# Attention scores of two experts side by side in 64-row TensorE tiles, without copied queries, in a decay-attention plus mixture-of-attention kernel

## The chip, the cores and the metric

The kernel runs on one core of one Trainium2 chip. A core has a matrix engine (TensorE, PE in the profile, with its weight loads shown as PEld), three elementwise engines (VectorE or DVE, ScalarE or ACT, GpSimd or POOL), a queue engine that here only issues transfers (SyncE or SP), an on-chip store of 128 partitions (SBUF) and eight accumulator banks of 128 partitions by 512 floats (PSUM). The metric is the device time of one launch in microseconds, as the median over runs. The time before is 322.6 us (three runs, 321.46 to 324.16).

## The reference, cut to what matters

```python
# 1. decay attention: 4 batches, 8 heads, 768 steps, 48 wide
for t in range(S):
    y[:, :, t] = rt @ (state + u * kt (x) vt)
    state = w * state + kt (x) vt
x = y as (4, 768, 384)
# 2. four experts of causal attention, 64 wide, two of four chosen per row
logits = x @ w_gate; topk = 2 best; w = softmax over them
for e in range(4):
    q, k, v = x @ wq[e], x @ wk[e], x @ wv[e]
    a = softmax(causal(0.125 * q @ k.T))
    out += [e in topk] * w_e * (a @ v @ wo[e])
```

Everything is float32. Where one TensorE pass at reduced precision would lose too much, the kernel splits a number into a rounded high part and the rest, a low part, and adds the products of the parts.

## The kernel before, in words

The 4 x 768 rows are cut into 24 chunks of 128 rows (n = 0 to 23). Three chunks make a group G (0 to 7, 384 rows); each batch has two groups, g = G % 2. The decay attention works by chunks (functions named a_...), the experts by groups (m_...).

For each chunk the decay attention ends in `a_add`, which leaves the 128 x 384 output. `a_xt` (lines 628 to 638) turns it on TensorE so that the 384 features lie on partitions: three columns of 128, read with a step of three floats, each in two halves of 64 rows (line 634, six transposes, the halves in two PSUM banks). ScalarE copies them out as the high part (line 637), and `a_xl` leaves the low part (line 645).

`m_proj(G, kind, pr)` (lines 666 to 698) computes queries (kind 0) or keys (kind 1) of the two experts 2 pr and 2 pr + 1 for a group: nine products of 384 columns (line 676), the first expert's 64 features on partitions 0 to 63, the second's on 64 to 127. Keys go to a tile of their own for each expert which holds the high part on the expert's own 64 partitions and the low part on the other 64: two copies on ScalarE (line 686) and two subtractions on VectorE (line 688), each on 64 partitions. Queries are split into high and low parts in the tile xq (lines 691 and 693), and then four transfers (line 698, on the SP queue) copy them so that each expert's query tile tq holds the same 64 features on both halves of the partitions.

`m_scores(G, e, j)` (lines 753 to 773) computes the scores of one expert for one chunk of queries against all N keys up to its end, N = 128 (3 g + j + 1). Because the key tile has high and low parts stacked, a single product over 128 partitions gives query x (high + low). It takes two: with the query's high part (line 763) and with its low part (line 764). For N of 640 and 768 each is cut into 384 columns and the rest. VectorE adds the causal mask and takes the row minimum in one instruction (line 770), and ScalarE takes the exponential and its sum (line 772). `m_weigh` scales the rows on GpSimd (line 785), `m_turn` turns them in halves of 64 rows (line 794), `m_av` multiplies by values (line 815), `m_out` projects to the output (lines 838 to 852). `m_values` (line 711) and `m_gate` give values and the gate.

Nothing here is scheduled while it runs. `ORDER` (line 16 on) is an order of the whole program written out: each word names a step and its arguments, and stands once for each stretch of that step between two `yield`s; the digits behind the slash say which buffers that stretch takes. The loop at line 863 goes through the words and issues the instructions in just that sequence, and each engine executes its own in that sequence. The eight PSUM banks are shared: `ps` number i is bank i, `psb` number i is banks i and i + 1 (`SHARED`, line 198).

Instructions on TensorE come in several shapes of the array: products over all 128 rows and 128 columns (lines 676, 711, 763, 764, 838 to 840), 64 rows by 128 columns (transposes in halves, lines 527, 634, 794), 64 by 64 (lines 566, 574, 599, 603) and 128 by 64 (line 815). The profile writes them as 128*128, 64*128, 64*64 and 128*64.

## Time and profile before

| | |
|---|---|
| median of three runs | 322.6 us (321.46 to 324.16) |
| the profiled execution's own time | 323.65 us |
| span of the profiled execution | 321.9 us |
| TensorE busy | 310.4 us (96%), 5406 products |
| VectorE, ScalarE, GpSimd busy | 214.8 us, 223.1 us, 174.3 us |
| transfers | 37.41 MB in 104698 packets |

Busy times overlap between engines. A product's record on TensorE is longer than the time it holds the engine, since the next one starts before the last has left the array; the pace of products that follow each other is therefore read from the distance between the ends of neighbours, or from the chain of waits, which counts each stretch once. Rows of a grouped view read: line, engine, operation, output and inputs, shape, count, then busy time and mean duration in ns, then idle time before them. Rows of the timeline read: start in us, length in us, engine, line, operation, count. Rows of the chain read: start, length, what.

### The profile page before, as it was taken

How to read it: one execution, taken by the hardware profiler on the slowest of the kernel's cores; microseconds unless marked ns; L12 is line 12 of the kernel's file. 1: busy time of each engine (PE TensorE's matmuls, PEld its weight loads, DVE VectorE, ACT ScalarE, POOL GpSimd, SP SyncE). 2: the span in 40 equal slices, each digit the busy share in tenths (PEclk: the TensorE clock that was granted, in tenths of full speed). 3: DMA queues.
4: the chain of work that ended last, by engine and by line, in shares of the span. 5: the costliest groups of instructions: out<-in, count | busy, mean ns of one | idle time of the engine just before them, and what ended most of it. 6: DMA issues, size and time to landing. Idle time of an engine off the chain costs nothing.

```text
span 321.9 us, 12990 instructions
## 1 busy us (share of the span) xinstructions
PE 310.4 (96%) x5406; PEld 264.7 (82%) x5407; DVE 214.8 (67%) x693; ACT 223.1 (69%) x525; POOL 174.3 (54%) x227
## 2 busy tenths in 40 slices
...
GB/s 168 223 176 104 100 197 115 148 178 170 117 82 180 180 57 119 195 134 2 150 108 152 53 126 70 166 190 73 77 89 100 170 27 4 124 145 30 25 51 73
DMA packets 104698, 37.41 MB, mean 116 GB/s; under 512 B 95550, under 2 KB 100544, under 8 KB 104640
## 3 DMA queue, kind: packets, MB, share of 16 engines
...
q14 instruction: 16, 0.13, 0.1%
q10 hardware_dynamic: 160, 0.10, 0.1%
...
## 4 chain that ended last, share of the span: by engine, by line
PE 89%; ACT 4%; DVE 3%; issue 2%; DMA 1%; ACTq 0%; DVEq 0%
PE banks L676 16%; PE banks L815 12%; PE banks L711 9%; PE banks L763 8%; PE banks L794 8%; PE banks L764 6%; PE banks L566 4%; PE banks L603 3%; PE banks L527 3%; PE banks L634 3%; PE banks L838 3%; PE banks L599 3%; PE banks L574 3%; PE banks L840 3%; PE banks L839 3%
## 5 line engine op out<-in xcount | busy, mean ns | idle before, releaser
L785 POOL TENSOR_SCALAR pr<-pr,f,gate 128x128 f32<-128x128 f32 (+5 forms) x96 | 67.8, 723 | 79.7 <-DVE f L779 35.6
L770 DVE CUSTOM_DVE_ANT_0 pr<-banks,after 128x256 f32<-128x256 f32 (+5 forms) x96 | 58.6, 620 | 37.2 <-PE banks L764 28.6
L772 ACT ACTIVATE pr<-pr,nm 128x384 f32<-128x384 f32 (+5 forms) x96 | 63.5, 663 | 19.9 <-DVE nm L770 17.9
L797 ACT ACTIVATE pt<-banks 128x768 f32<-128x768 f32 (+1 forms) x64 | 44.5, 729 | 8.5 <-PE banks L794 8.3
L763 PE MATMUL banks<-tk,tq 128*128 128x384 f32 (+3 forms) x128 | 45.0, 355 | 0.1
L815 PE MATMUL banks<-pt,vv 128*64 128x384 f32 (+2 forms) x324 | 40.4, 393 | 1.0 <-DVE yl L824 0.7
L764 PE MATMUL banks<-tk,tq 128*128 128x384 f32 (+3 forms) x128 | 40.4, 322 | 0.0
L815 PEld LDWEIGHTS banks<-pt,vv 128*64 128x64 f32 x324 | 20.6, 136 | 17.5 <-issue 12.8
L676 PE MATMUL banks<-xt_hi,wqk_lo 128*128 128x384 f32 x96 | 32.5, 338 | 0.5 <-issue 0.5
L676 PE MATMUL banks<-xt_hi,wqk_hi 128*128 128x384 f32 x96 | 32.9, 342 | 0.0
L794 PEld LDWEIGHTS banks<-ident,pr 64*128 64x128 f32 x672 | 24.7, 139 | 9.5 <-issue 4.4
L676 PE MATMUL banks<-xt_lo,wqk_hi 128*128 128x384 f32 x96 | 32.3, 336 | 0.0
L794 PE MATMUL banks<-ident,pr 64*128 64x64 f32 x672 | 30.2, 229 | 0.8 <-ACT pt L797 0.6
L626 POOL TENSOR_TENSOR z<-z,w 128x192 f32<-128x192 f32 x20 | 10.2, 509 | 34.5 <-DVE z L622 34.5
L763 PEld LDWEIGHTS banks<-tk,tq 128*128 128x128 f32 x128 | 24.0, 187 | 3.7 <-ACT vv L716 0.3
L490 POOL TENSOR_TENSOR rdbuf<-rdbuf,tab_r 128x384 f32<-128x384 f32 x22 | 23.1, 1053 | 7.1 <-DMA rdbuf<-in_r_dram 5.1
L497 POOL TENSOR_TENSOR ku<-kdbuf,uw 128x384 f32<-128x384 f32 x24 | 25.0, 1046 | 0.4
L490 POOL TENSOR_TENSOR kdbuf<-kdbuf,tab_k 128x384 f32<-128x384 f32 x21 | 22.3, 1063 | 5.3 <-DMA kdbuf<-in_k_dram 5.2
L499 POOL TENSOR_TENSOR ku<-ku,rdbuf 128x384 f32<-128x384 f32 x24 | 24.5, 1023 | 1.3
L599 PE MATMUL banks<-vsbuf,sm 64*64 64x48 f32 x384 | 23.9, 220 | 0.5 <-issue 0.3
L764 PEld LDWEIGHTS banks<-tk,tq 128*128 128x128 f32 x128 | 24.1, 188 | 0.3
L599 PE MATMUL banks<-vhbuf,sm 64*64 64x48 f32 x384 | 23.9, 219 | 0.0
...
## 6 DMA issues: line engine op xcount, KB each, us to landing
tq<-xq SPq DMA_DIRECT2D x64, 192.0 KB, 3.4
kdbuf<-in_k_dram SPq DMA_DIRECT2D x24, 192.0 KB, 3.6
vhbuf<-in_v_dram SPq DMA_DIRECT2D x24, 192.0 KB, 3.8
rdbuf<-in_r_dram SPq DMA_DIRECT2D x24, 192.0 KB, 3.7
out_dram<-o SPq DMA_DIRECT2D x23, 192.0 KB, 2.5
...
pr<-in_moe_wo_dram SPq DMA_DIRECT2D x2, 192.0 KB
...
```

Of the source, the lines that this page charges most:

```text
L490: nc.gpsimd.tensor_tensor(t[:, :, :D], t[:, :, :D], (tab_k, tab_r)[which], op=OP.mult)
L599: nc.tensor.matmul(o, st["sm", n][par][rows, p // 2, i], values, start=fresh, stop=True)
L676: nc.tensor.matmul(ps, a[:, t, m0:m0 + P], x[:, t, :], start=i == 0, stop=i == n - 1)
L711: nc.tensor.matmul(ps, x[:, t, cols], a[:, t, :], start=m == 0, stop=m == n - 1)
L763: nc.tensor.matmul(o, tq[:, 0, q], keys[:, n0:n1], start=True, stop=False)
L764: nc.tensor.matmul(o, tq[:, 1, q], keys[:, n0:n1], start=False, stop=True)
L770: nc.vector.tensor_tensor_reduce(pr[:, :N], ps, after[:, S - N:], 1.0, 3e38, op0=OP.add, op1=OP.min, accum_out=nm)
L772: nc.scalar.activation(pr[:, :N], pr[:, :N], AF.Exp, bias=nm, scale=-1.0, accum_out=sums[:, e, j, 0:1])
L785: nc.gpsimd.tensor_scalar(p[:, :N], p[:, :N], f[:, i], gate[:, i, e:e + 1], op0=OP.mult, op1=OP.mult)
L794: nc.tensor.transpose(both[:, x, half], mg[G]["p", e, j][rows, i * C:(i + 1) * C], ident[rows, rows])
L797: nc.scalar.activation(pt.rearrange("s (x half c) -> s x half c", x=n, half=2), both, AF.Copy)
L815: nc.tensor.matmul(psy[par * HD:par * HD + HD, j0 * C:j1 * C], vv[:, i % GC, e, :], mg[G]["t", e, i][:, (j0 - max(0, i - g * GC)) * C:(j1 ...
```

## The change

`m_scores` now takes a pair of experts at once. Keys and queries keep the layout in which `m_proj` leaves them, the pair's experts on the two halves of the partitions, with high and low parts as two tiles side by side. For each stretch of keys there are three products for each expert (high x high, high x low, low x high; low x low is dropped), each over 64 partitions, and those of the two experts alternate, each expert writing to its own bank or pair of banks. The four transfers for queries and the tile xq are gone, and keys take one copy and one subtraction over 128 partitions in place of two each over 64. `a_xt` turns the whole 128 rows at once, three transposes into one bank. There are eight probability tiles in place of six and three query tiles (of a pair) in place of four (of an expert). The order of the whole program is laid anew; of its text only the end is shown here, then all of the rest of the diff.

```diff
--- before.py
+++ after.py
...
-m_turn,7,0,0/4 m_av,6,0,0,3/1 m_scores,7,1,0/0 m_av,6,0,0,3/0 m_out,5,1/0 m_turn,7,0,0/3 m_scores,7,1,0/14
-m_scores,7,1,0 m_scores,7,1,1/1 m_scores,7,1,1/05 m_scores,7,1,1 m_proj,7,0,1/31 m_scores,7,2,2/6 m_out,5,0 m_proj,7,1,1
-m_turn,7,0,1/4 m_turn,7,0,2/0 m_turn,7,0,1/2 m_weigh,7,1/1 m_weigh,7,1 m_av,6,1,0,3/2 m_av,6,1,0,3/0 m_scores,7,2,0/3
-m_scores,7,2,2/43 m_scores,7,2,1/5 m_turn,7,0,2/0 m_av,6,1,0,3/1 m_out,6,0/7 m_scores,7,2,2 m_turn,7,1,0/0
-m_scores,7,2,1/11 m_scores,7,2,1 m_turn,7,1,0/5 m_turn,7,1,1/5 m_turn,7,1,1/1 m_scores,7,2,0/02 m_out,6,0/1
-m_scores,7,3,0/4 m_scores,7,3,2/2 m_turn,7,1,2/0 m_scores,7,3,2/44 m_out,5,1 m_scores,7,2,0 m_scores,7,3,0/50
-m_scores,7,3,2 m_out,6,0 m_weigh,7,2/2 m_out,6,2/5 m_weigh,7,2 m_scores,7,3,1/6 m_scores,7,3,0 m_out,6,1/2
-m_scores,7,3,1/25 m_scores,7,3,1 m_weigh,7,3/0 m_weigh,7,3 m_av,7,0,0,3/3 m_turn,7,1,2/4 a_sum,17 m_turn,7,2,1/0
-m_out,6,1/0 m_out,6,1 m_turn,7,2,0/6 m_out,6,2/1 m_turn,7,2,1/3 m_turn,7,2,0/5 m_av,7,0,3,6 m_av,7,0,3,6/1
-m_turn,7,3,0/4 m_turn,7,3,2/6 m_turn,7,3,1/0 m_turn,7,3,0/0 m_turn,7,2,2/4 m_turn,7,3,1/2 m_turn,7,2,2/4 m_turn,7,3,2/1
-m_av,7,1,3,6/1 m_av,7,1,3,6/0 m_av,7,0,3,6/1 m_av,7,1,3,6/0 m_out,7,0/3 m_av,7,1,3,6 m_av,7,1,3,6 m_out,7,1/7 m_out,6,2
-m_av,7,1,3,6 m_out,7,0/0 m_out,7,1/1 m_av,7,1,3,6 m_out,7,2/2 m_out,7,0 m_out,7,1 m_out,7,2/1 m_out,7,2/0 m_out,7,2/1
-m_out,7,2
...
+m_turn,6,3,0/4 m_gate,7/300 m_proj,7,1,0 m_proj,7,0,1/0 m_proj,7,0,1 m_gate,7 m_scores,7,0,0/03 m_scores,7,0,0/46
+m_scores,7,0,0/35 m_scores,7,0,1/16 m_turn,6,3,0/2 m_out,5,0/0 m_scores,7,0,1/54 m_scores,7,0,1/21 m_scores,7,0,2/31
+m_scores,7,0,2/02 m_weigh,6,2 m_turn,6,2,0/5 m_scores,7,0,0 m_scores,7,0,0 m_scores,7,0,1 m_out,5,1/7 m_out,5,0/1
+m_scores,7,0,2/50 m_turn,6,2,0/1 m_out,4,0 m_scores,7,0,2 m_scores,7,0,2 m_gate,7/600 m_weigh,7,0/0 m_out,5,2/0
+m_scores,7,0,1 m_weigh,7,1/3 m_proj,7,1,1/2 m_proj,7,1,1 m_out,5,0 m_av,6,0,0,3/3 m_out,5,1/0 m_out,5,1 m_out,5,2/1
+m_av,6,0,0,3/0 m_proj,7,1,1 m_scores,7,1,2/64 m_weigh,7,0 m_weigh,7,1 m_turn,7,0,1/0 m_turn,7,0,1/5 m_av,6,1,0,3/2
+m_scores,7,1,2/23 m_scores,7,1,2/57 m_scores,7,1,2 m_av,6,0,0,3/0 m_turn,7,0,0/6 m_turn,7,1,1/0 m_turn,7,0,0/1
+m_turn,7,1,1/4 m_scores,7,1,0/45 m_turn,7,0,2/6 m_turn,7,0,2/0 m_av,6,1,0,3/1 m_turn,7,1,0/0 m_scores,7,1,0/16
+m_scores,7,1,0/42 m_scores,7,1,0 m_av,6,1,0,3/1 m_scores,7,1,1/63 m_out,6,1/5 a_sum,5 m_turn,7,1,0/3 m_scores,7,1,1/34
+m_scores,7,1,1/05 m_out,6,0/1 m_scores,7,1,1 m_out,5,2 m_scores,7,1,0 m_scores,7,1,1 m_out,6,2/2 m_weigh,7,2/2
+m_weigh,7,2 m_turn,7,1,2/6 m_av,7,0,0,3/0 m_scores,7,1,2 m_weigh,7,3/3 m_weigh,7,3 m_out,6,0/0 m_turn,7,2,0/3
+m_turn,7,1,2/2 m_out,6,1/1 m_out,6,1 m_turn,7,2,0/1 m_turn,7,2,1/6 m_turn,7,2,1/3 m_av,7,0,3,6 m_av,7,0,3,6/1
+m_turn,7,3,0/3 m_turn,7,3,0/0 m_turn,7,3,1/5 m_turn,7,3,1/2 m_turn,7,3,2/3 m_av,7,0,3,6/0 m_turn,7,2,2/0 m_out,6,0
+m_turn,7,3,2/4 m_turn,7,2,2/5 m_av,7,1,3,6/7 m_out,6,2/1 m_av,7,1,3,6/0 m_av,7,1,3,6/1 m_out,7,0/5 m_av,7,1,3,6
+m_out,7,0/0 m_out,6,2 m_out,7,0 m_av,7,1,3,6 m_av,7,1,3,6 m_out,7,1/2 m_out,7,1/1 m_av,7,1,3,6 m_out,7,1 a_sum,17
+m_out,7,2/7 m_out,7,2/1 m_out,7,2/3 m_out,7,2/1 m_out,7,2
 """
 
 BUFS = {
-    "ps": 8, "psb": 7, "pr": 6, "tq": 4, "xq": 2, "pt": 6, "yh": 2, "yl": 2, "ku": 2, "ownv": 2, "kt": 2, "rt": 3, "rx": 3, "sm": 4, "z": 3, "o": 2,
+    "ps": 8, "psb": 7, "pr": 8, "tq": 3, "pt": 6, "yh": 2, "yl": 2, "ku": 2, "ownv": 2, "kt": 2, "rt": 3, "rx": 3, "sm": 4, "z": 3, "o": 2,
     "tk": 2, "vv": 3, "xt_hi": 2, "xt_lo": 2, "lg": 2, "gt": 2, "dl": 2, "ex": 2,
     "gate": 2, "nm": 6, "f": 4,
 }
 WIDTH = {
-    "ps": 512, "psb": 1024, "pr": 768, "tq": 768, "xq": 768, "pt": 768, "yh": 384, "yl": 384, "ku": 384, "ownv": 384,
+    "ps": 512, "psb": 1024, "pr": 768, "tq": 768, "pt": 768, "yh": 384, "yl": 384, "ku": 384, "ownv": 384,
     "kt": 512, "rt": 512, "rx": 256, "sm": 256, "z": 576, "o": 384, "tk": 3072, "vv": 768, "xt_hi": 1152, "xt_lo": 1152, "lg": 12, "gt": 48,
     "dl": 12, "ex": 12, "gate": 12, "nm": 1, "f": 3,
 }
 SHARED = {"ps": 512, "psb": 512}
-ROUNDED = ("tq", "xq", "yh", "yl", "tk", "xt_hi", "xt_lo")
+ROUNDED = ("tq", "yh", "yl", "tk", "xt_hi", "xt_lo")
 
 EARLY = 3
 
@@ -628,21 +616,19 @@
     def a_xt(n):
         G, j = divmod(n, GC)
         x = st["x", n]
-        ps = take("psb").rearrange("s (half x) -> s half x", half=2)[:, :, :KT * 64].rearrange("s half (t c) -> s t half c", t=KT)
+        ps = take("ps")[:, :KT * C].rearrange("s (t c) -> s t c", t=KT)
         for t in range(KT):
-            for half, rows in enumerate((lo, hi)):
-                nc.tensor.transpose(ps[:, t, half], x.rearrange("s (p t) -> s p t", t=KT)[rows, :, t], ident[rows, rows])
+            nc.tensor.transpose(ps[:, t, :], x.rearrange("s (p t) -> s p t", t=KT)[:, :, t], ident)
         cols = slice(j * C, (j + 1) * C)
         yield
-        nc.scalar.activation(turned("xt_hi", G)[:, :, cols].rearrange("s t (half c) -> s t half c", half=2), ps, AF.Copy)
+        nc.scalar.activation(turned("xt_hi", G)[:, :, cols], ps, AF.Copy)
         st["xt", n] = ps
 
     def a_xl(n):
         G, j = divmod(n, GC)
         hi, lo = turned("xt_hi", G), turned("xt_lo", G)
         cols = slice(j * C, (j + 1) * C)
-        halves = (x[:, :, cols].rearrange("s t (half c) -> s t half c", half=2) for x in (lo, hi.bitcast(F32)))
-        nc.vector.tensor_tensor(next(halves), st["xt", n], next(halves), op=OP.subtract)
+        nc.vector.tensor_tensor(lo[:, :, cols], st["xt", n], hi[:, :, cols].bitcast(F32), op=OP.subtract)
 
 
     sumsbuf = [const.tile([P, E, GC, 2], F32, name=f"sums{i}") for i in range(2)]
@@ -653,15 +639,14 @@
 
     mg = {G: {} for G in range(B * NG)}
 
-    def keys_of(G):
-        b, g = divmod(G, NG)
-        return get("tk", b).rearrange("s (e g c) -> s e g c", e=E, g=NG)[:, :, g]
+    def keys_of(b, pr):
+        return get("tk", b).rearrange("s (p i c) -> s p i c", p=E // 2, i=2)[:, pr]
 
     def values_of(G):
         return get("vv", G).rearrange("s (j e h) -> s j e h", j=GC, e=E)
 
-    def query_of(G, e):
-        return get("tq", G, e).rearrange("s (i c) -> s i c", i=2)
+    def query_of(G, pr):
+        return get("tq", G, pr).rearrange("s (i c) -> s i c", i=2)
 
     def m_proj(G, kind, pr):
 
@@ -676,26 +661,16 @@
                 nc.tensor.matmul(ps, a[:, t, m0:m0 + P], x[:, t, :], start=i == 0, stop=i == n - 1)
                 i += 1
         yield
-        top, bot = slice(0, 64), slice(64, 128)
         if kind:
-
-            tk = keys_of(G)
-            for e, own, other in ((2 * pr, top, bot), (2 * pr + 1, bot, top)):
-                if e % 2:
-                    yield
-                nc.scalar.activation(tk[own, e, :], ps[own], AF.Copy)
-                yield
-                nc.vector.tensor_tensor(tk[other, e, :], ps[own], tk[own, e, :].bitcast(F32), op=OP.subtract)
+            x2 = keys_of(b, pr)[:, :, g * GT:(g + 1) * GT]
+            nc.scalar.activation(x2[:, 0], ps, AF.Copy)
+            yield
+            nc.vector.tensor_tensor(x2[:, 1], ps, x2[:, 0].bitcast(F32), op=OP.subtract)
             return
-        x2 = take("xq").rearrange("s (i c) -> s i c", i=2)
+        x2 = query_of(G, pr)
         nc.scalar.activation(x2[:, 0], ps, AF.Copy, scale=-scale)
         yield
         nc.vector.scalar_tensor_tensor(x2[:, 1], ps, -scale, x2[:, 0].bitcast(F32), op0=OP.mult, op1=OP.subtract)
-        yield
-        for e, half in ((2 * pr, top), (2 * pr + 1, bot)):
-
-            for rows in (top, bot):
-                nc.sync.dma_start(query_of(G, e)[rows].bitcast(F32), x2[half].bitcast(F32))
 
     def logits_of(G):
         return get("lg", G).rearrange("p (c e) -> p c e", c=GC)
@@ -750,27 +725,28 @@
         nc.vector.tensor_tensor(gate, den.to_broadcast([P, GC, E]), ex, op=OP.mult)
         mg[G]["gate"] = gate
 
-    def m_scores(G, e, j):
+    def m_scores(G, pr, j):
         b, g = divmod(G, NG)
-        tq, sums = query_of(G, e), sumsbuf[G % 2]
+        tq, tk, sums = query_of(G, pr), keys_of(b, pr), sumsbuf[G % 2]
         N = (g * GC + j + 1) * C
-        psb = take("psb")
         q = slice(j * C, (j + 1) * C)
-        keys = get("tk", b).rearrange("s (e c) -> s e c", e=E)[:, e]
         first = 0 if N <= 512 else 512 - GT
+        ps = [take("ps" if N <= 512 else "psb")[:, first:first + N] for _ in range(2)]
         for n0, n1 in ((0, N),) if N <= 512 else ((0, GT), (GT, N)):
-            o = psb[:, first + n0:first + n1]
-            nc.tensor.matmul(o, tq[:, 0, q], keys[:, n0:n1], start=True, stop=False)
-            nc.tensor.matmul(o, tq[:, 1, q], keys[:, n0:n1], start=False, stop=True)
-        ps = psb[:, first:first + N]
-        yield
-
-        nm = take("nm")
-        pr = take("pr")
-        nc.vector.tensor_tensor_reduce(pr[:, :N], ps, after[:, S - N:], 1.0, 3e38, op0=OP.add, op1=OP.min, accum_out=nm)
-        yield
-        nc.scalar.activation(pr[:, :N], pr[:, :N], AF.Exp, bias=nm, scale=-1.0, accum_out=sums[:, e, j, 0:1])
-        mg[G]["p", e, j] = pr
+            for i, (part, key) in enumerate(((0, 0), (0, 1), (1, 0))):
+                for par, rows in enumerate((lo, hi)):
+                    nc.tensor.matmul(ps[par][:, n0:n1], tq[rows, part, q], tk[rows, key, n0:n1], start=i == 0, stop=i == 2)
+        prs = []
+        for par in range(2):
+            yield
+            nm, pr_ = take("nm"), take("pr")
+            nc.vector.tensor_tensor_reduce(pr_[:, :N], ps[par], after[:, S - N:], 1.0, 3e38, op0=OP.add, op1=OP.min, accum_out=nm)
+            prs.append((nm, pr_))
+        for par, (nm, pr_) in enumerate(prs):
+            yield
+            e = 2 * pr + par
+            nc.scalar.activation(pr_[:, :N], pr_[:, :N], AF.Exp, bias=nm, scale=-1.0, accum_out=sums[:, e, j, 0:1])
+            mg[G]["p", e, j] = pr_
 
     def m_weigh(G, e):
         g = G % NG
```

More of the change, by code (lines that the diff above doesn't have):

```diff
@@ new lines @@
+a_decay,11,0 a_quarters,9/4 a_sum,8/2 a_sum,9 m_scores,1,1,1 m_scores,1,1,1 a_sum,9/0 load_chunk,12 m_proj,2,1,0/7
+a_mask,9/03 a_sum,10 m_proj,2,1,0/1 a_ku,10/1 a_ku,10 load_vs,9 a_out,9 load_vs,12 load_chunk,13 load_chunk,13
+m_weigh,1,3/0 a_out,10 m_weigh,1,2/3 m_weigh,1,2 m_weigh,1,3 m_proj,2,0,1/3 m_proj,2,0,1/2 m_proj,2,1,1/6 a_own,10/0
+a_add,10 load_vh,13 a_xt,10/5 load_chunk,11 m_proj,2,1,0 a_add,9 m_proj,2,1,1 a_xt,9/2 a_decay,12,1 m_proj,2,1,1
+a_xt,9/1 a_xl,9/1 m_proj,2,0,0/1 a_xt,10 m_av,1,0,0,3/7 m_proj,2,0,1 m_turn,1,3,2/1 load_chunk,14 m_turn,1,3,2/3 a_ku,12
@@ new lines @@
+m_scores,2,1,2/05 m_scores,2,1,2/57 m_weigh,2,1/1 a_xt,11 a_xt,12/0 a_xt,12/0 a_decay,14,1 a_decay,14,0 a_transpose,14/2
+a_transpose,13/5 m_av,1,1,3,6/0 a_xl,12/0 a_transpose,14/0 a_decay,15,0 m_av,1,1,3,6/1 m_out,1,2/7 a_decay,15,1 a_xl,11
+m_proj,3,0,0/4 a_transpose,13/1 a_transpose,13/00 m_out,1,2/0 a_sum,11 m_weigh,2,1 m_turn,2,1,0/0 m_weigh,2,0/1
+m_weigh,2,0 m_turn,2,0,0/5 a_transpose,14/21 m_values,3,0/7 m_scores,2,1,1/23 m_scores,2,1,1/13 load_vh,14
+m_turn,2,1,0/3 load_chunk,16 a_decay,16,0 a_ku,14/1 a_ku,14 m_turn,2,0,0/1 m_values,3,0/0 load_chunk,16
@@ new lines @@
+m_turn,3,1,2/6 m_scores,3,1,1/46 m_proj,4,0,1/4 m_scores,3,1,1/32 m_out,2,0 m_scores,3,1,1 a_decay,19,1 m_weigh,3,2/3
+a_xt,15/2 m_proj,4,1,1 m_turn,3,1,2/5 load_vh,18 a_ku,16 a_xt,15/1 a_own,16/71 m_values,4,2/0 m_values,4,0/3
+m_values,4,0 m_scores,3,1,1 a_xl,15/1 m_values,4,2 m_values,4,2 m_out,2,2/1 m_out,0,0 m_proj,4,0,1/1 a_quarters,16/2
+m_proj,4,0,1 a_transpose,18/5 m_gate,4/000 m_scores,3,1,0 m_scores,3,1,2 m_weigh,3,3/1 m_av,3,0,0,3/4 a_sum,15/2
+load_chunk,20 a_sum,16 a_mask,16/31 m_values,4,0 m_out,2,2/1 a_ku,17/0 m_gate,4 m_gate,4/311 a_transpose,18/0
@@ new lines @@
+a_transpose,18/11 m_weigh,3,2 m_av,3,0,3,6 m_av,3,0,3,6/1 m_av,3,0,3,6/0 a_out,16 m_turn,3,2,2/0 a_ku,18/1
+m_turn,3,2,2/2 m_weigh,3,3 m_turn,3,2,1/5 m_turn,3,2,1/4 warm_up m_turn,3,3,0/3 m_turn,3,3,0/1 m_scores,4,0,1/10
+a_add,16 a_xt,16/7 a_xt,16 m_turn,3,3,2/5 m_turn,3,3,2/0 m_scores,4,0,1/51 m_scores,4,0,1/13 a_sum,16/1 m_turn,3,3,1/1
+m_turn,3,3,1/3 a_decay,20,0 m_turn,3,2,0/3 m_scores,4,0,0/05 a_xl,16 a_decay,17,1 a_transpose,17/6 a_ku,17
+m_scores,4,0,0/42 m_scores,4,0,0/25 m_scores,4,1,2/12 m_scores,4,1,2/37 m_scores,4,0,2/05 m_scores,4,0,2/00
```

277 lines of the change are left out of this document (121 added, 156 removed).

## The prediction

> **What bounds the kernel now.** I read the head of the page first, then busy time by stretches, then the chain of waits.
>
> ```profile
> span 321.9 us, 12990 instructions
> PE 310.4 (96%) x5406; PEld 264.7 (82%) x5407; DVE 214.8 (67%) x693; ACT 223.1 (69%) x525; POOL 174.3 (54%) x227
> PE 89%; ACT 4%; DVE 3%; issue 2%; DMA 1%; ACTq 0%; DVEq 0%
> PE banks L676 16%; PE banks L815 12%; PE banks L711 9%; PE banks L763 8%; PE banks L794 8%; PE banks L764 6%; PE banks L566 4%; PE banks L603 3%; PE banks L527 3%; PE banks L634 3%; PE banks L838 3%; PE banks L599 3%; PE banks L574 3%; PE banks L840 3%; PE banks L839 3%
> ```
>
> ```profile
> 12.00:40.00 28.00, 24.73 (x655) 21.88 (x655) 23.67 (x57) 20.79 (x49) 23.12 (x23) 1.00 0.64 144
> 40.00:312.00 272.00, 268.99 (x4646) 230.27 (x4645) 183.57 (x609) 197.14 (x466) 146.73 (x185) 1.00 0.50 113
> ```
>
> In the second view the columns after the length are PE, PEld, DVE, ACT, POOL busy, then the granted clock. From 40 to 312 us TensorE stands idle for 272.00 - 268.99 = 3.0 us; the next engine, ScalarE, is busy for 197 of 272. The chain agrees: 89% of it is TensorE. So work taken from TensorE shortens the span almost one for one, and work taken from VectorE, ScalarE or the transfers does nothing directly. The scores (lines 763 and 764) are 14% of the chain.
>
> **What a product costs.** Busy times overlap, so I take paces: the distance between the ends of neighbours in the timeline, and chain rows divided by their counts.
>
> ```profile
> 47.93 0.23 PE L763 MATMUL banks<-tk,tq 128*128 128x128 f32 x1
> 47.99 0.28 PE L764 MATMUL banks<-tk,tq 128*128 128x128 f32 x1
> ...
> 50.09 0.56 PE L634 MATMUL banks<-ident,ownv 64*128 64x64 f32 x6
> 50.57 0.39 PE L763 MATMUL banks<-tk,tq 128*128 128x256 f32 x1
> 50.80 0.28 PE L764 MATMUL banks<-tk,tq 128*128 128x256 f32 x1
> ```
>
> ```profile
> 299.08 0.35 PE L794 MATMUL banks<-ident,pr 64*128 64x64 f32 x6
> 299.36 0.50 PE L763 MATMUL banks<-tk,tq 128*128 128x512 f32 x1
> 299.70 0.40 PE L764 MATMUL banks<-tk,tq 128*128 128x512 f32 x1
> ```
>
> ```profile
> 60.43 1.57 PE banks L676 x9
> ...
> 63.95 0.50 PE banks L527 x16
> ...
> 66.69 0.52 PE banks L794 x12
> ```
>
> A product of 384 columns takes 1.57 / 9 = 0.174 us; of 512, from 299.86 to 300.10, 0.24; of 256, from 50.96 to 51.08, 0.12; of 128, from 48.16 to 48.27, 0.11. The last is as dear as twice its columns, so below 256 columns the weight load sets a floor of 0.11 for a step.
>
> A change of array shape costs more. At 50.57 the array goes from 64*128 to 128*128: from the end before (50.09 + 0.56 = 50.65) to that of the first product (50.96) is 0.31 against 0.12 for the next, 0.19 more. At 299.36 it is 0.43 against 0.24, again 0.19. Into 64*128: twelve transposes after L676 take 0.52, while sixteen within the shape take 0.50, or 0.031 each; 0.52 - 12 x 0.031 = 0.15.
>
> [...]
>
> **Scores.** By the code, each batch and expert has N = 128, 256, 384, 512, 384 + 256 and 384 + 384, two products each. Over 4 batches and 4 experts that is 128 products of 384 columns, 64 of 256, 32 of 128, 32 of 512: 128 x 0.174 + 64 x 0.12 + 32 x 0.11 + 32 x 0.24 = 22.3 + 7.7 + 3.5 + 7.7 = 41.2 us. Afterwards a pair needs three steps where it needed four products; if the two experts' products run side by side in their halves of the rows, and a step costs what a whole product of that width does, it is 96, 48, 24 and 24 steps, 30.9 us. Gain 10.3.
>
> Does a pair run side by side? The trace has no such product at reduced precision, but it has other work in halves and quarters of the array:
>
> ```profile
> 10.65 0.87 PE banks L407 x8
> ...
> 57.64 0.62 PE banks L566 x32
> ```
>
> ```profile
> L566 PEld LDWEIGHTS banks<-rt,kt 64*64 64x64 f32 x768 | 13.8, 134 | 3.1 <-issue 0.8 <-DVE kdbuf L488 0.5 <-DVE ownv L508 0.3
> L676 PEld LDWEIGHTS banks<-xt_hi,wqk_hi 128*128 128x128 f32 x96 | 18.0, 188 | 0.6 <-ACT vv L716 0.2
> ```
>
> A whole transpose of 128 x 128 takes 0.87 / 8 = 0.109; in two halves it takes 2 x 0.031 = 0.062, which two halves in turn, 0.054 each by their columns, would not reach. Ordinary products in quarters come every 0.62 / 32 = 0.019, under a quarter of the width's cost. In both the halves of the rows write to different banks, as the new scores do. So I take side by side. Bounds: nothing gained or lost per column (side by side, 30.9) and all in turn, 2 x 30.9 = 61.8; the nearest rows are near the first end.
>
> **Changes of shape.** Scores move from the whole shape to the one of the transposes in halves; `a_xt` the other way. I walked through both written orders and noted the shape of each step that issues to TensorE. Before: 67 changes into 128*128 (43 of them at scores), 63 into 64*128, 34 into 64*64, 18 into 128*64. Afterwards: 55, 59, 37, 19 (scores cause 19, `a_xt` 14, `m_proj` 13 instead of 3). 12 x 0.19 + 4 x 0.15 - 4 x 0.15 = 2.3; with the column shape, whose price I don't separate, 2.2 gained, bounds 1.8 to 2.5.
>
> **Turning whole.**
>
> ```profile
> 49.27 0.43 PEld L634 LDWEIGHTS banks<-ident,ownv 64*128 64x128 f32 x6
> ```
>
> ```profile
> L634 PEld LDWEIGHTS banks<-ident,ownv 64*128 64x128 f32 x144 | 10.2, 202 | 2.7 <-DVE ownv L610 0.7 <-issue 0.4 <-DVE tk L688 0.3
> L794 PEld LDWEIGHTS banks<-ident,pr 64*128 64x128 f32 x672 | 24.7, 139 | 9.5 <-issue 4.4 <-POOL pr L785 2.8 <-POOL kdbuf L490 0.6
> ```
>
> The six loads of a chunk come in three pairs, (0.43 - 0.20) / 2 = 0.12 apart, although the same transposes on contiguous data (L794) pace at 0.062 a pair: the load with a step of three floats, 0.202 long against 0.139, sets the pace. A whole transpose needs the same load once, and its own 0.109 can hide behind the next load, as loads hide in the run of L407. I take three steps of 0.12, as before: nothing. Bounds: 0.11 each (24 x 0.03 = 0.7 gained), and load and transpose end to end, 0.12 + 0.11 = 0.23 each, 24 x 3 x 0.11 = 7.9 lost; the overlap in L407 decides for the first.
>
> **Edits with no price.**
>
> ```profile
> L686 ACT ACTIVATE tk<-banks 64x384 fp32r<-64x384 f32 x32 | 15.2, 484 | 8.1 <-PE banks L676 7.0 <-DVE tk L688 0.6
> L688 DVE TENSOR_TENSOR tk<-banks,tk 64x384 fp32r<-64x384 f32 x32 | 17.4, 554 | 5.6 <-ACT tk L686 5.0
> L691 ACT ACTIVATE xq<-banks 128x384 fp32r<-128x384 f32 x16 | 7.8, 485 | 3.9 <-PE banks L676 3.7
> ```
>
> ```profile
> tq<-xq SPq DMA_DIRECT2D x64, 192.0 KB, 3.4
> ```
>
> A copy over 128 partitions (0.485) costs what one over 64 does (0.484), so keys lose 16 copies and 16 subtractions, 7.7 us of ScalarE and 8.9 of VectorE. The 64 query transfers go, with 3.4 us of latency each between projection and scores. All of this lies beside TensorE, which had 3.0 us of idle time to give; without that cover it would be worth at most those 3. In the new order the nearest scores (7,1,2) follow their projection with one `m_av` between, longer than the 0.485 + 0.554 that the split needs.
>
> **Waits of the new order.** The other engines keep 96% of their work while TensorE loses 4%, and a step of scores now fills two banks, or four, which one VectorE must empty.
>
> ```profile
> L770 DVE CUSTOM_DVE_ANT_0 pr<-banks,after 128x768 f32<-128x768 f32 x16 | 15.3, 956 | 7.4 <-PE banks L764 5.1 <-ACT pt L797 1.9 <-PE banks L794 0.4
> L770 DVE DVE_READ_ACCUMULATOR2_ANT nm<- 128x1 f32 x96 | 8.0, 83 | 0.0
> ```
>
> The second expert's banks are free 0.956 + 0.083 = 1.04 us later than the first's. I add half of the present idle time, 1.5 us; bounds -1.5 and 16.6 (all sixteen pairs of 640 and 768 keys wait that 1.04).
>
> **Sum.** -10.3 - 2.2 + 0 + 1.5 = -11.0 against the profiled execution's 323.65 us (span 321.9 and 1.75 around it): 312.65. That execution was 1.05 above the median of the runs, so for the median I forecast 311.6 us.
>
> **Rivals.**
>
> *Stalls at the banks* (0.14). The order may be tighter than its words show. Half of the 16.6 above, 8 us, gives 311.6 + 8 = 319.6. For: a pair of 640 or 768 keys takes four of eight banks, and two more are held by the values' sums. Against: VectorE was busy for 184 of 272 us and loses 8.9.
>
> *Weight loads exposed* (0.08), the one that ends slower. In each half of the rows the load for the next step would wait until the half's product is done. A step then costs load plus stream: 0.174 + 0.11 for 384, 0.23 for 256, 0.058 (a third of 0.174) + 0.11 for 128, 0.35 for 512, so 96 x 0.284 + 48 x 0.23 + 24 x 0.168 + 24 x 0.35 = 50.7 us of scores, 9.5 more than now; -2.2 + 1.5 besides gives 311.6 + 19.8 = 331.4. It decides as soon as a step of 384 columns costs over 0.26. Against: L676 paces at 0.174 with loads of 0.188 over the same rows, and L527 at 0.062 a pair, so loads hide behind products there. [...]
>
> *Halves in turn* (0.05). Reduced-precision products of two halves don't overlap: 61.8 us of scores, 311.6 + 30.9 = 342.5. For: no row shows such a product; against: L566 and L527.
>
> *Loads in turn* (0.05), the case in which the change does not bring what it says. The two loads of a step follow each other: a floor of 2 x 0.11 = 0.22 a step, 168 x 0.22 + 24 x 0.24 = 42.7, no gain over 41.2; 311.6 + 11.8 = 323.4. Against: L566 loads last 0.134 and come every 0.019.
>
> **How the numbers follow.** The forecast has 0.68, its own range 307 (more of the drains saved, no new waits, transposes at 0.11) to 315 (3 us more of waits). The range for 8 in 10 takes in the stalls and part of the dear transposes (up to 319.5): 307 to 321. About 1% is what a measurement of this kernel can tell from no change, so the lines are at 319.4 and 325.8. Faster: 0.68 and half of the stalls, 0.07, 0.75; same: the other half and loads in turn, 0.05, 0.12; slower: 0.08 + 0.05 = 0.13.
>
> **What would show it.** Right: steps of a pair of scores start together and pace at 0.17 to 0.18 for 384 columns; the score lines' share of the chain falls to about 10%; TensorE idle in the middle stays under 5 us; `a_xt` takes 0.33 to 0.37 us a chunk without its drain; 170 drains of 0.15 to 0.19 us remain. Wrong: a pace of 0.28 or 0.35, transposes at 0.23, or more than 10 us of TensorE idle before scores, named as waits for VectorE.

## The result, and the profile after

| | before | after |
|---|---|---|
| median of the runs taken together on one chip | 322.1 us (321.46 to 324.16) | 310.24 us (309.75 to 310.41) |
| profiled execution, own time | 323.65 us | 310.19 us |
| its span | 321.9 us | 308.5 us |

The ratio of the times (of their means) is 0.9619, with a 95% interval of 0.9572 to 0.9665. The forecast was 311.6 us with a range of 307 to 321. Runs of one kernel differ with the clock that TensorE was granted (the kernel before, run beside the experiments, took 321.64 us at a mean clock of 1.0 and 324.93 at 0.989), and where the runs of an experiment lie further apart than that, its ratio is that of the shorter ones.

The head of the page after, then the chain by engine and by line, which answer to the first fence of the prediction:

```profile
span 308.5 us, 12933 instructions
PE 298.6 (97%) x5463; PEld 253.6 (82%) x5463; DVE 202.8 (66%) x677; ACT 213.7 (69%) x509; POOL 173.8 (56%) x227
PE 90%; ACT 6%; issue 1%; DMA 1%; DVE 1%; ACTq 0%; DVEq 0%
PE banks L661 17%; PE banks L791 12%; PE banks L738 11%; PE banks L686 9%; PE banks L770 7%; PE banks L554 4%; PE banks L591 4%; PE banks L587 4%; PE banks L515 4%; PE banks L621 4%; PE banks L814 3%; PE banks L562 3%; PE banks L816 3%; PE banks L815 3%; ACT pt L773 2%
```

The span fell by 13.4 us. TensorE is busy for 11.8 us less (310.4 to 298.6), and its idle time, span less busy, fell from 321.9 - 310.4 = 11.5 us to 308.5 - 298.6 = 9.9 us. Scores are now line 738, with 11% of the chain in place of 14%. Busy time by stretches (TensorE first, then its weight loads, VectorE, ScalarE, GpSimd, granted clock):

```profile
12.00:40.00 28.00, 25.83 (x719) 23.14 (x709) 24.43 (x62) 20.34 (x48) 23.35 (x26) 1.00 0.45 100
40.00:298.00 258.00, 256.06 (x4638) 218.31 (x4636) 170.81 (x589) 186.99 (x449) 146.58 (x185) 1.00 0.34 74
```

In the middle 1.9 us of idle time are left, where there were 3.0; between 12 and 40 us, 2.2 where there were 3.3. TensorE is still the bound.

The new scores. First the timeline of one pair of experts with 768 keys (two stretches of 384 columns), then three rows of the chain around it:

```profile
76.90 0.41 PE L770 MATMUL banks<-ident,pr 64*128 64x64 f32 x8
77.13 1.29 PE L738 MATMUL banks<-tk,tq 64*128 64x384 f32 x12
```

```profile
76.80 0.52 PE banks L770 x12
77.32 1.10 PE banks L738 x12
78.42 0.55 PE banks L621 x3
```

The first row of the chain's three is transposes, the next that pair's scores (12 products, six steps). Six steps in 1.10 us are 0.183 each. In the records of the single products, the two of a step start 3 to 4 ns apart (77.126 and 77.129, 77.384 and 77.388, ...; the median over all steps is 4 ns), and from the second step on the ends of the steps are 0.173 to 0.177 us apart. Grouped over the whole trace the median pace is 0.17 for 384 columns, 0.116 for 256, 0.11 for 128 and 0.234 for 512: the four figures of the forecast, within 0.006.

The split of the keys (lines 666 and 668), and the transfers of the whole kernel after:

```profile
L666 ACT ACTIVATE tk<-banks 128x384 fp32r<-128x384 f32 x16 | 7.8, 485 | 5.2 <-PE banks L661 5.2
L668 DVE TENSOR_TENSOR tk<-banks,tk 128x384 fp32r<-128x384 f32 x16 | 8.8, 548 | 3.5 <-ACT tk L666 3.5
DMA packets 99578, 24.83 MB, mean 81 GB/s; under 512 B 94526, under 2 KB 99520, under 8 KB 99520
```

Sixteen copies and sixteen subtractions are left, and 12.6 MB of transfers are gone, as the code says.

### The profile page after: what moved, and what is told of

Read it like the earlier page. It is cut to its first block, busy times and chain, and to the rows that moved or that the text cites. A ratio compares the mean times of both kernels' runs of the same rounds, so it can differ in the third digit from the quotient of the medians.

```text
span 308.5 us, 12933 instructions
## 1 busy us (share of the span) xinstructions
PE 298.6 (97%) x5463; PEld 253.6 (82%) x5463; DVE 202.8 (66%) x677; ACT 213.7 (69%) x509; POOL 173.8 (56%) x227
## 4 chain that ended last, share of the span: by engine, by line
PE 90%; ACT 6%; issue 1%; DMA 1%; DVE 1%; ACTq 0%; DVEq 0%
PE banks L661 17%; PE banks L791 12%; PE banks L738 11%; PE banks L686 9%; PE banks L770 7%; PE banks L554 4%; PE banks L591 4%; PE banks L587 4%; PE banks L515 4%; PE banks L621 4%; PE banks L814 3%; PE banks L562 3%; PE banks L816 3%; PE banks L815 3%; ACT pt L773 2%
## 5 line engine op out<-in xcount | busy, mean ns | idle before, releaser
L743 DVE CUSTOM_DVE_ANT_0 pr<-banks,after 128x384 f32<-128x384 f32 (+5 forms) x96 | 56.3, 621 | 38.9 <-PE banks L738 33.3
L748 ACT ACTIVATE pr<-pr,nm 128x256 f32<-128x256 f32 (+5 forms) x96 | 63.3, 662 | 15.5 <-DVE nm L743 14.0
L738 PE MATMUL banks<-tk,tq 64*128 64x384 f32 (+3 forms) x384 | 42.0, 338 | 0.2 <-ACT pt L773 0.2
L738 PEld LDWEIGHTS banks<-tk,tq 64*128 64x128 f32 x384 | 31.1, 185 | 4.3 <-ACT pt L773 0.8
L791 PEld LDWEIGHTS banks<-pt,vv 128*64 128x64 f32 x324 | 20.5, 136 | 16.2 <-issue 11.8
L661 PE MATMUL banks<-xt_hi,wqk_hi 128*128 128x384 f32 x96 | 33.7, 351 | 0.1
L485 POOL TENSOR_TENSOR ku<-kdbuf,uw 128x384 f32<-128x384 f32 x24 | 24.3, 1017 | 16.4 <-DVE banks L494 16.2
L478 POOL TENSOR_TENSOR kdbuf<-kdbuf,tab_k 128x384 f32<-128x384 f32 x21 | 21.3, 1023 | 11.3 <-DMA kdbuf<-in_k_dram 6.4
L614 POOL TENSOR_TENSOR z<-z,w 128x192 f32<-128x192 f32 x20 | 10.9, 545 | 27.2 <-DVE z L610 24.9
L686 PE MATMUL banks<-wv_hi,xt_hi 128*128 128x260 f32 x72 | 21.7, 302 | 0.0
L686 PE MATMUL banks<-wv_hi,xt_lo 128*128 128x260 f32 x72 | 20.5, 285 | 0.0
```

What stands on the lines that cost most here:

```text
L478: nc.gpsimd.tensor_tensor(t[:, :, :D], t[:, :, :D], (tab_k, tab_r)[which], op=OP.mult)
L485: nc.gpsimd.tensor_tensor(ku, kd[:, :, :D], uw, op=OP.mult)
L661: nc.tensor.matmul(ps, a[:, t, m0:m0 + P], x[:, t, :], start=i == 0, stop=i == n - 1)
L686: nc.tensor.matmul(ps, x[:, t, cols], a[:, t, :], start=m == 0, stop=m == n - 1)
L738: nc.tensor.matmul(ps[par][:, n0:n1], tq[rows, part, q], tk[rows, key, n0:n1], start=i == 0, stop=i == 2)
L743: nc.vector.tensor_tensor_reduce(pr_[:, :N], ps[par], after[:, S - N:], 1.0, 3e38, op0=OP.add, op1=OP.min, accum_out=nm)
```

## The experiments

Times below are set against runs of the kernel before, taken together with them on the same chip. The median of those was 322.9 to 323.7 us there, so a difference from the kernel after is worked out from the ratios: (ratio - 0.9619) x 322 us. With the intervals of both ratios it is known to about 2 us; the plain difference of the times is up to 1.2 us larger. The diffs are cut to the lines that matter: declarations, and lines that only follow from the ones shown, are left out.

### Four whole products in the new order

```diff
-            for i, (part, key) in enumerate(((0, 0), (0, 1), (1, 0))):
-                for par, rows in enumerate((lo, hi)):
-                    nc.tensor.matmul(ps[par][:, n0:n1], tq[rows, part, q], tk[rows, key, n0:n1], start=i == 0, stop=i == 2)
+            for par in range(2):
+                for part in range(2):
+                    nc.tensor.matmul(ps[par][:, n0:n1], tq[:, part, q], tk[:, 0, n0:n1], start=part == 0, stop=part == 1)
```

> The changed kernel with its order, buffers and lack of query copies, but the scores of a pair as four products over all 128 rows (as many columns as before the change) in place of three pairs of 64-row products. Both experts' rows are mixed in each product, so the scores are not the reference's. Theory (the gain is the pairing): 41.2 us of score stream instead of 30.9, and by the written order 15 more changes of array shape at 0.15 to 0.19 us, 2.6 us: 310.2 + 10.3 + 2.6 = 323 us, no better than the kernel before the change. Rival (the new order, the freed buffers and the missing transfers bring most of it): 312 to 316 us.

Measured: 318.4 us, ratio 0.9864 (0.9825 to 0.9902), so 7.9 us more than after. The page shows the work at line 738 coming back:

```profile
PE 308.0 (97%) x5334; PEld 263.1 (83%) x5335; DVE 204.0 (64%) x677; ACT 214.1 (68%) x509; POOL 174.4 (55%) x227
PE banks L661 17%; PE banks L738 14%; PE banks L791 12%; PE banks L686 9%; PE banks L770 7%; PE banks L554 4%; PE banks L591 4%; PE banks L515 4%; PE banks L587 3%; PE banks L562 3%; PE banks L814 3%; PE banks L621 3%; PE banks L816 3%; PE banks L815 3%; ACT pt L773 1%; DMA ownv<-in_w_dram 1%
```

TensorE is busy for 308.0 - 298.6 = 9.4 us more. Neither theory had the number: about 8 us come from the pair side by side and about 4.5 from the rest of the change. Summed by line from the ends of the records, scores take 49.6 us before, 46.4 here and 37.2 after. The first step, 3.2 us, goes with fewer changes of shape ahead of scores: 44 before, 26 here. But the records count 181 changes of shape in all in both kernels: what left the scores stands ahead of other steps now (`m_proj` 10 in place of 3, `a_transpose` 18 in place of 11). By the ends of the records these took little or nothing more (52.4 us against 52.0, and 15.8 against 16.0), while TensorE's idle time fell from 11.5 us to 316.9 - 308.0 = 8.9. So which part of the rest of the change brings the 4.5 us is not settled by this run.

### The two experts' products in turn

```diff
-            for i, (part, key) in enumerate(((0, 0), (0, 1), (1, 0))):
-                for par, rows in enumerate((lo, hi)):
+            for par, rows in enumerate((lo, hi)):
+                for i, (part, key) in enumerate(((0, 0), (0, 1), (1, 0))):
```

> The changed kernel with the two loops of the score products exchanged: all three products of the first expert, then all three of the second, so that neighbours in the queue use the same half of the rows. Nothing else changes. Theory (halves run side by side, and only neighbours in different halves can): of six products only the third and fourth overlap, five steps instead of three, 30.9 x 5 / 3 = 51.5 us of stream, 20.6 more: about 331 us. Rival (a 64-row product is simply cheaper by itself, or products of different halves overlap at any distance): within 3 us of 310.

Measured: 310.16 us, ratio 0.9611 (0.957 to 0.9652): no difference from after. The theory that only neighbours overlap fell; which half of the rival holds, the next run decides. The same pair's row in the timeline:

```profile
76.69 1.29 PE L738 MATMUL banks<-tk,tq 64*128 64x384 f32 x12
```

It has the same 1.29 us as in the kernel after, although three products of one half now stand ahead of three of the other. In the records they again start in pairs, here 3 to 4 ns apart (76.692 and 76.695, 76.951 and 76.954, ...); the median over all steps is 10 ns.

### All six products in one half of the rows

```diff
-                    nc.tensor.matmul(ps[par][:, n0:n1], tq[rows, part, q], tk[rows, key, n0:n1], start=i == 0, stop=i == 2)
+                    nc.tensor.matmul(ps[par][:, n0:n1], tq[lo, part, q], tk[lo, key, n0:n1], start=i == 0, stop=i == 2)
```

> The changed kernel with the second expert's score products reading the first expert's queries and keys, partitions 0 to 63, so that all six products of a step lie in one half of the rows; instructions, widths and banks are the same. The second expert of each pair gets the first one's scores. After the run with exchanged loops it is open whether a 64-row product is half as dear by itself, or whether each half of the rows has a queue of its own and the two run beside each other. Theory (two queues): nothing overlaps here, 61.8 us of stream in place of 30.9, about 341 us. Rival (a 64-row product is cheaper by itself): 310 us.

Measured: 337.64 us, ratio 1.0456 (1.0406 to 1.0506), 27 us more than after, near the 31 of the theory; the rival fell. Group of products of 384 columns, after and then here:

```profile
L738 PE MATMUL banks<-tk,tq 64*128 64x384 f32 x192 | 23.7, 355 | 0.2 <-ACT pt L773 0.2
```

```profile
L738 PE MATMUL banks<-tk,tq 64*128 64x384 f32 x192 | 39.3, 344 | 0.3 <-ACT pt L773 0.2
```

The same products of the same shape, 355 and 344 ns long, cover 39.3 us in place of 23.7. A product over half of the rows is no cheaper than a whole one: the twelve of a pair with 768 keys have a row of 2.35 us in the timeline here, where six steps side by side have 1.29, so six more take 1.06, or under 0.18 each, against 0.174 for a whole product. What the pairing gains is that the other half's product runs beside it.

### Eighty changes of shape more

A small transpose in the 64*64 shape ahead of each `m_proj` and each `m_values`, to columns of the bank that nothing reads (shown for `m_proj`; `m_values` has the same):

```diff
-        ps = take("ps")[:, :GT]
+        bank = take("ps")
+        nc.tensor.transpose(bank[:64, GT:GT + 64], ident[:64, :64], ident[:64, :64])
+        ps = bank[:, :GT]
```

> The changed kernel with one 64 x 64 transpose of the identity into unused bank columns before each of the 56 projections and value products, which adds 80 changes of array shape by the written order (48 into 64*64, 32 into 128*128). Theory (a change costs 0.14 to 0.19 us of TensorE time wherever it stands): 48 x 0.14 + 32 x 0.19 = 12.8 us more, 323 us. Rival (a change of shape is mostly hidden, and the records only show it): under 314 us.

Measured: 324.51 us, ratio 1.0026 (0.9998 to 1.0053), 13.1 us more than after: 13.1 / 80 = 0.16 us for a change of shape, its small transpose included (the records show 78 more changes, which gives 0.17). That is inside the prediction's 0.15 to 0.19, and the rival that a change is mostly hidden fell.

### Turning whole in the kernel before

```diff
-        for t in range(KT):
-            for half, rows in enumerate((lo, hi)):
-                nc.tensor.transpose(ps[:, t, half], x.rearrange("s (p t) -> s p t", t=KT)[rows, :, t], ident[rows, rows])
+        for t in range(KT):
+            nc.tensor.transpose(ps[:, t, :], x.rearrange("s (p t) -> s p t", t=KT)[:, :, t], ident)
```

> The kernel before the change with one part of the change alone: the decay outputs are turned whole, three transposes in place of six halves. Theory (the strided weight load sets the pace of 0.12 us either way): the stream is the same, and by the written order there are 5 changes of array shape fewer, 0.9 us: 321 us, within 1 us of before. Rival (load and transpose end to end, 0.23 us each): 24 x 3 x 0.11 = 7.9 us more, 329 us.

Measured: 321.83 us, ratio 0.9975 (0.9945 to 1.0005): no difference that can be told from none, so the rival's 7.9 us fell. The records count 176 changes of shape in place of 181, five fewer as expected. In the kernel after the chain has single chunks and neighbouring ones:

```profile
47.60 0.90 PE banks L621 x6
...
65.60 0.55 PE banks L621 x3
```

Three more transposes cost 0.90 - 0.55 = 0.35 us, 0.12 each, the prediction's step; the other 0.2 of the 0.55 is the change of shape.

### Keys in halves again

```diff
-            nc.scalar.activation(x2[:, 0], ps, AF.Copy)
+            for rows in (lo_, hi_):
+                nc.scalar.activation(x2[rows, 0], ps[rows], AF.Copy)
             yield
-            nc.vector.tensor_tensor(x2[:, 1], ps, x2[:, 0].bitcast(F32), op=OP.subtract)
+            for rows in (lo_, hi_):
+                nc.vector.tensor_tensor(x2[rows, 1], ps[rows], x2[rows, 0].bitcast(F32), op=OP.subtract)
```

> The changed kernel with the 16 key copies and 16 subtractions that the change saved put back, in halves of 64 partitions; no transfers. Theory (VectorE and ScalarE work lies beside TensorE; the 40 us of the run with transfers came from the SP queue): 310 us, within 1.5 us. Rival (they were part of it): 313 us or more.

Measured: 314.23 us, ratio 0.973 (0.9678 to 0.9782), 3.6 us more than after. The rival held: this work isn't free in the new order. Busy time over the span, then by stretches, then waits of TensorE, with the microseconds, the times and the longest:

```profile
PE 301.5 (96%) x5462; PEld 255.2 (82%) x5463; DVE 212.2 (68%) x693; ACT 222.0 (71%) x525; POOL 174.1 (56%) x227
...
40.00:298.00 258.00, 255.32 (x4580) 217.33 (x4580) 178.85 (x603) 191.38 (x458) 146.16 (x185) 1.00 0.34 73
...
PE banks L741 <- DVE tk L671: 0.7, 1, 0.7
```

Scores now wait for the split of the keys, which costs no wait worth listing in the kernel after; idle time in this stretch is 2.7 us in place of 1.9. It has not all gone into one wait, and most of it isn't idle time: over the span TensorE is busy for 2.9 us more (301.5 against 298.6) with the same products, and idle for 312.4 - 301.5 = 10.9 us, 1.0 more. A product of 384 columns has a record of 0.33 to 0.36 us and the next follows 0.174 later, so a wait shorter than that overlap lengthens the busy time and leaves no gap. By the ends of the records scores take 38.8 us in place of 37.2, `a_quarters` (lines 554 and 562) 27.1 in place of 26.1.

### Query copies back, four ways

The 64 query transfers of 192 KB, in four forms. First each expert's 64 rows to both halves behind the split of the queries, to a tile that nobody reads (with the keys in halves as well):

```diff
         nc.vector.scalar_tensor_tensor(x2[:, 1], ps, -scale, x2[:, 0].bitcast(F32), op0=OP.mult, op1=OP.subtract)
+        for half in (lo_, hi_):
+            for rows in (lo_, hi_):
+                nc.sync.dma_start(copied[0][rows].rearrange("s (i c) -> s i c", i=2), x2[half].bitcast(F32))
```

> The changed kernel with the work that the change took from the other engines put back: each key tile is copied and subtracted in two halves of 64 partitions (16 copies and 16 subtractions more), and four transfers of 192 KB follow each query split on the SP queue, to a tile that nobody reads. The results are the changed kernel's. Theory (all of it lies beside TensorE): 310 us, within 1 us. Rival (the freed queue and engines are part of the gain): 313 us or more.

Measured: 349.84 us, ratio 1.0852 (1.0792 to 1.0912), 40 us more than after: the theory fell, by far more than the rival asked for. Waits of the SP queue, then of TensorE:

```profile
SPq L679 <- DVE tq L676: 48.6, 6, 16.0
SPq L679 <- DMA copied<-tq: 37.7, 35, 3.7
...
PE banks L587 <- DMA vsbuf<-in_v_dram: 8.7, 2, 8.1
PE banks L694 <- DVE nm L751: 5.9, 1, 5.9
```

The order was laid without these transfers, and the SP queue takes its instructions in turn: for 48.6 us, in six waits of up to 16.0, it stood at a transfer whose queries weren't ready, and chunk loads stood behind. Another 37.7 us it stood at a transfer whose predecessor hadn't landed, since here all of them write one tile. So much of the price can be that of a place in a queue and not of the bytes, and a run without such waits has to show it. So the second form puts them late, in the second stretch of `m_weigh`, when the queries have long been there:

```diff
+        for rows in (lo, hi):
+            nc.sync.dma_start(copied[rows].rearrange("s (i c) -> s i c", i=2), query_of(G, e // 2)[(lo, hi)[e % 2]].bitcast(F32))
```

> The changed kernel with the 64 query transfers put back on the SP queue, two for each expert, but issued after its scores are weighed, when the queries have long been split, so that the SP queue does not wait for them; they go to a tile that nobody reads. Theory (the transfers' bytes are free, and what cost 40 us was the SP queue standing at a transfer whose queries were not ready, with the chunks' loads behind it): 310 to 312 us. Rival (the traffic itself slows loads or the matrix engine): 318 us or more.

Measured: 333.49 us, ratio 1.0316 (1.0253 to 1.0379). This didn't isolate the traffic either. Waits of ScalarE, then of SP:

```profile
ACT tq L671 <- DMA copied<-tq: 13.4, 3, 7.0
```

```profile
SPq L763 <- DMA copied<-tq: 26.7, 23, 3.3
```

ScalarE, which writes the next queries into the same buffer, waits up to 7.0 us for a transfer still to come that reads the old ones, and TensorE stops for 6.5 us at 64.7 us and for 4.1 us at 110.6.

The third form keeps place and size and takes the queries away: the source is a constant tile.

```diff
+        for rows in (lo, hi):
+            nc.sync.dma_start(copied[rows], after[(lo, hi)[e % 2]])
```

> The kernel after, with 64 transfers of 192 KB put back at the same places as in the run with late query copies, but reading a constant tile, so that no engine waits for one to have read the queries. If the bytes and the issues of those transfers are free (the prediction's price of nothing), ratio 0.960 to 0.966, some 310 to 312 us. If the traffic itself costs, because chunk loads then arrive later, TensorE shows waits for kdbuf, rdbuf or vsbuf and the ratio is at 0.985 or above (318 us and more).

Measured: 323.93 us in the middle of ten runs (319.26 to 328.34), ratio 0.9937 (0.9891 to 0.9984) from the five under 324 us: some 10 us more than after, which looks like a price of the traffic. The trace of one of these five (322.43 us) says otherwise. Its SP queue around 72 us in the timeline, then the wait of TensorE over the whole span, then busy time by stretches around the first stall:

```profile
70.51 0.97 SPq L311 DMA_DIRECT2D vsbuf<-in_v_dram  x1
71.52 5.35 SPq L763 DMA_DIRECT2D copied<-after  x4
76.92 0.65 SPq L311 DMA_DIRECT2D vsbuf<-in_v_dram  x1
```

```profile
PE banks L587 <- DMA vsbuf<-in_v_dram: 4.9, 2, 3.0
```

```profile
76.00:80.50 4.50, 1.53 (x84) 1.33 (x83) 1.84 (x7) 0.49 (x1) 4.50 (x6) 1.00 0.51 109
80.50:81.50 1.00, 1.00 (x56) 0.95 (x58) 0.00 (x0) 0.00 (x0) 1.00 (x2) 0.99 0.00 0
81.50:85.50 4.00, 4.00 (x31) 3.56 (x31) 2.35 (x5) 1.22 (x2) 2.12 (x3) 0.58 0.62 119
```

Two `m_weigh` follow each other closely, their transfers write the same rows, so the later ones wait for the earlier, and the load of vsbuf queued behind them is issued at 76.92. TensorE stops for 3.0 us at 77.4, and from 81.5 to 84.9 it has half its clock, which is worth another 1.7 us. At 214.6 us the same half clock of 3.4 us follows the second stall, of 1.9 us. So 4.9 + 2 x 1.7 = 8.3 us are two late loads and what followed, of the 10 us by the ratio, or of the 12 by which this execution is longer than the profiled one after.

The last form takes this wait away, with a place of its own for each transfer, off the chip:

```diff
+        for rows in (lo, hi):
+            nc.sync.dma_start(copied[G, e, rows], after[(lo, hi)[e % 2]])
+
+    copied = nc.dram_tensor("copied", (B * NG, E, P, 768), F32, kind="Internal").ap()
```

> The kernel after, with 64 transfers of 192 KB at the same places as in the run with the constant tile, but each to a place of its own in memory off the chip, so that no transfer waits for an earlier one and the SP queue is not held up. If the 10 us of that run came from the SP queue standing behind such waits (two late vsbuf loads, two stalls of TensorE of 3 us, and the half clock of 3.4 us that followed each), they go: ratio 0.960 to 0.966, 310 to 312 us, and the granted clock is 1.0 in the middle. If the bytes or the issues themselves cost, vsbuf, kdbuf or rdbuf still come late: ratio 0.975 or above (315 us and more).

Measured: 314.32 us (311.91 to 315.41), ratio 0.971 (0.9635 to 0.9785): between the two theories, 2.9 us more than after by the middle, with an interval that overlaps that of after. The queue's bytes, the longest wait for a load, and the middle stretch:

```profile
DMA packets 104698, 37.42 MB, mean 120 GB/s; under 512 B 95550, under 2 KB 100544, under 8 KB 104640
...
PE banks L587 <- DMA vsbuf<-in_v_dram: 1.2, 1, 1.2
PE banks L587 <- issue: 1.1, 1, 1.1
...
40.00:298.00 258.00, 254.19 (x4576) 216.81 (x4574) 170.59 (x588) 182.98 (x443) 145.67 (x184) 1.00 0.52 121
```

With all 37.4 MB of the kernel before on the queue, most of the 10 us are gone and the granted clock is 1.00 again. One vsbuf load still comes 1.2 us late, and line 587 stands once more, for 1.1 us, without a named cause. In this form the copies go to memory off the chip and not to another tile, and their median from issue to landing is 3.6 us where it was 3.1 in the third form, so their landing isn't the same; what the issue and the bytes cost by themselves is 0 to 5 us by the interval of this ratio, near 3, and can't be told from nothing.

### The words of the order moved

The same instructions and buffers, the words moved within what data and buffers allow, 184 of 1350 by more than five places, so that steps stand nearer to where their data is ready; an excerpt:

```diff
-load_vh,15 m_scores,3,0,1/12 m_scores,3,0,2 a_quarters,15/50 m_proj,3,0,1/2 m_gate,3 m_gate,3/110 m_turn,2,3,0/4
+load_vh,15 m_scores,3,0,2 m_gate,3 m_scores,3,0,1/12 m_scores,3,0,1 m_gate,3/110 m_scores,3,0,1 m_turn,2,3,0/4
```

> The kernel after with the words of its order moved within what the data and the named buffers allow; the same instructions, the same buffers, about the same number of changes of shape (169). What is left to gain is waits alone. If the theory holds that the kernel after has some 2 us of idle time from 40 to 298 us, 2 us from 12 to 40 and 4 us in the last 12, it gains 1 to 4 us: ratio 0.950 to 0.959. The rival, that the written order already meets the waits as they are and moving words only makes new ones, has 0.960 to 0.975.

Measured: 315.29 us, ratio 0.9741 (0.9708 to 0.9774), 3.9 us more than after. The rival held: in this move, the only one tried, the written order already met its waits. Changes of shape are the same 168 in the records of both. The middle and the end by stretches:

```profile
40.00:298.00 258.00, 254.99 (x4560) 216.09 (x4554) 171.60 (x586) 182.59 (x441) 145.16 (x184) 1.00 0.34 73
298.00:313.40 15.40, 10.36 (x132) 8.58 (x126) 1.79 (x5) 6.24 (x15) 1.21 (x2) 0.96 0.19 65
```

TensorE is idle for 3.0 us in the middle (1.9 after), and in what follows 298 us for 15.4 - 10.4 = 5.0 us in place of 3.8. The rest is in busy time again: 301.3 us over the span in place of 298.6, with the same 5463 products. No version here beats the kernel after.

## Why the prediction was right, and the step that failed

The forecast of the median was 1.4 us too high, that of the profiled execution 2.5 (312.65 against 310.19). The prediction's terms in order:

**What bounds the kernel: right.** The span fell by 13.4 us, TensorE's busy time by 11.8 and its idle time by 1.6.

**Scores side by side: right in its mechanism.** The paces are those of the forecast, and the two experiments that bear on it agree: without the second half of the rows the kernel takes 27 us more, with whole products 8 more. But of its 12.5 us for scores and changes of shape (10.3 + 2.2), 11.8 came. By the prediction's own prices scores would go from 41.2 + 43 x 0.19 = 49.4 us (49.6 measured) to 30.9 + 19 x 0.15 = 33.8, where 37.2 were measured. Three terms make up most of the 3.4. A change of shape into the new scores costs 0.19 and not 0.15: the first step of 384 columns after one takes 0.368 against 0.174 for the next, 19 x 0.04 = 0.8. Where scores follow transposes within the same shape, which I had at nothing, the first step takes 0.228, 20 x 0.054 = 1.1. And three steps waited, at 0.305, 0.484 and 0.628 us, 0.9 together: each was released by a ScalarE instruction that empties a bank (line 773 twice, line 538 once), so these are waits of the new order that the records show as busy time. That the two terms came within 0.7 us all the same is partly luck. By the same prices all other lines would have grown by 3.1 us, from changes of shape that moved to them (`m_proj` 13 in place of 3); by the ends of the records, which count idle time too, they went from 267.4 us to 266.4, with 1.6 us less of idle time, so they grew by about 0.6. Turning probabilities, for one, takes 27.1 us (27.9 before) and values 28.5 (28.9).

**Changes of shape: right.** 181 in the records of before, 168 after, where I had counted 182 and 170; 0.16 us for one where eighty were added. What the forecast's range and its signs call a drain is such a change; the traces show its time, 0.15 to 0.19 us in the kernel before, and not what TensorE does in it. That these changes were worth 2.2 us in this kernel isn't shown by itself: with whole products in the new order there were 181 again, and the kernel was still 4.5 us faster than before.

**Turning whole at nothing: right**, with the step of 0.12; that the load sets it was argued from its 0.202 us against 0.139, and no run tests it. The chunk takes 0.35 us beside its change of shape, as forecast.

**Edits with no price: not shown to be right.** I named the cover, TensorE's idle time, and at most 3 us without it. Put back into the new order, the keys' second copies cost 3.6 us and the transfers near 3. But moving words alone, with no work added, cost 3.9. So in the new order work that it wasn't laid for, or words moved from their places, cost 3 to 4 us in these runs (the transfers perhaps nothing), while exchanging the two loops of the scores cost nothing; what the removed work had cost in the order of before, which was laid with it, stays open.

**Waits of the new order, +1.5: this step failed, in its sign.** I took a second expert's banks coming free 1.04 us later as new waits. Idle time fell by 1.6 us instead, from 11.5 to 9.9, and this isn't one execution's chance: it is 11.1 in the trace with outputs turned whole before, and 9.8 in the one with the two experts' products in turn. In the list of TensorE's idle waits after, scores stand once, and not for a VectorE instruction of line 743:

```profile
PE banks L738 <- ACT pt L773: 0.2, 1, 0.2
```

A weight load of scores waits for line 743 once, for 0.2 us. VectorE itself waits for 39 us before that line and works for 203 of 308 us. So the banks were late at three steps, by the 0.9 us above, and it was ScalarE that released them; other waits too short to leave a gap are not separated here. What made idle time fall stays open: the lighter ScalarE and VectorE (9.4 and 12.0 us less of work), the SP queue without its 64 transfers, and the new order all changed at once. It isn't the pairing of products, since with whole products in the new order idle time is 8.9 us.

**The rivals.** *Stalls at the banks*, *loads in turn* and *halves in turn* fell with the paces. *Weight loads exposed* would have shown a step of 0.28; it is 0.174 with a load of 0.184 in each half. Each half streams its six steps without a gap, 0.173 to 0.177 us from one end to the next, and so does the lower half alone, with 2.35 us for twelve products; a load of 0.184 in a step of 0.174 overlaps a running product of its own rows. The 0.08 was the author's estimate, and no row of the traces speaks for this rival. That the 0.11 us of a step of 128 columns is set by its weight load was an inference from 0.11 against the 0.12 of 256 columns; no run varies the load alone, and after the change the step still takes 0.11.
